# Two output-projection loads moved ahead of the last V load in a decode kernel bound by its loads

## Chip, cores, metric

The kernel runs on one core of one Trainium2 chip. The metric is the device time of one execution in microseconds (us); a profile gives the span of one execution, which is about 1.3 us shorter than the time.

## The reference

One token goes through one transformer block: adaptive layer norm, attention of 32 query heads over 4 cached K/V heads of 65,536 positions in the reference (128 wide), output projection, and a gated feed-forward.

```python
mod = (_silu(c) @ w_mod).reshape(...)              # sa, ca, ga, sb, cb, gb
h = _layernorm(x) * (1 + ca) + sa
x = x + ga * attention(h, k_cache, v_cache, wq, wo)
h = _layernorm(x) * (1 + cb) + sb
x = x + gb * ((gelu(h @ w_gate) * (h @ w_up)) @ w_down)
```

With one token, every weight and every cache row is used once. The profile counts 185.6 MB read, of which 134 MB are the caches (32 loads of 4,096 KB). How fast these bytes come in is the main question of this kernel.

## The kernel before

The kernel keeps ten slots of 16 KB per partition in on-chip memory. A K or V load (4,096 KB, two chunks of 64 positions per partition) takes two neighbouring slots: K loads take turns on slots 0 to 3, V loads on slots 4 to 7. Slots 8 and 9 carry weights only, before and after the attention. The loads are planned as one list. One engine (SyncE) issues them strictly in the order of that list, each once its slots have been freed:

```python
def issue_ready():
    while issued[0] < len(loads):
        j = loads[issued[0]]
        if any(q.freed[t] is None for q, t in j.prev):
            return
        SP.wait(*(q.freed[t] for q, t in j.prev))        # the slots' former readers are done
        sp.dma_start(j.view, j.src).then_inc(j.tok[0], 16)
        issued[0] += 1
# ... cut ...
for i in range(0, NC + UN, UN):                          # NC = 32 chunks, UN = 2 per load
    if i < NC:
        j_k[i] = plan_load(kv_src(kh, i, UN), ..., i % SITES, ...)
    if i >= UN:
        j = i - UN
        j_v[j] = plan_load(kv_src(vh, j, UN), ..., SITES + j % SITES, ...)
tail = iter([8, 9, 0, 1, 2, 4, 3, 5, 6, 7, 8, 9] + [0, 1, 2, 4, 3, 5, 6, 7])
j_o = [(plan_load(wo_v[:, k:k + 8, :], flat(8, D), next(tail)), k, 8) for k in range(0, HQ, 8)]
# ... then w_gate (4 loads), w_up (4), w_down (3 large, 3 small) on the next slots of tail
```

So the last V load comes behind the last K load and the V load before it, and it needs slots 6 and 7, which the value products (PV) of chunks 26 and 27 must free. Everything behind it in the list waits too. At the end come the merging of the chunks' softmax, the product with wo, a layer norm, and the feed-forward's three products. Each of these takes its weights load by load.

## Time and profile before

| | before |
|---|---|
| time, first three runs | 445.17 us median (444.18 to 446.75) |
| profiled execution | 444.85 us, span 443.5 us |
| load queue q1, share of 16 DMA engines' span | 97.9% |
| TensorE (PE) busy | 72% |

These lines of the page of the kernel before give the span, the mean busy share of the DMA engines in 40 slices of 11.1 us (in tenths), what they moved in each slice, and the queues (packets, MB, share):

```profile
span 443.5 us, 16706 instructions
...
DMA  8999999999999999999999999999999899999995
GB/s 328 430 423 425 451 424 433 434 429 428 426 431 429 434 441 427 431 434 431 429 446 429 429 434 432 429 443 432 429 437 429 358 378 421 419 425 421 426 426 217
...
q1 hardware_dynamic: 10864, 185.60, 97.9%
q8 instruction: 25, 0.41, 0.3%
```

The queue is full nearly everywhere. Of the inner slices only the 32nd and 33rd are low, with 358 and 378 GB/s. The next fence cuts that place into windows of 2 us. The columns are busy time (instructions) per engine, then the granted clock of PE, the busy share of the DMA engines, and GB/s:

```profile
core 0: us, PE busy (x) PEld busy (x) DVE busy (x) ACT busy (x) POOL busy (x), PEclk, DMA share, GB/s
350.00:352.00 2.00, 2.00 (x49) 2.00 (x46) 1.07 (x2) 0.00 (x0) 0.00 (x0) 0.66 0.95 410
352.00:354.00 2.00, 2.00 (x67) 2.00 (x64) 1.80 (x2) 0.00 (x0) 0.00 (x0) 1.00 0.57 246
354.00:356.00 2.00, 2.00 (x50) 1.88 (x48) 0.45 (x2) 1.92 (x2) 0.00 (x0) 1.00 0.36 98
356.00:358.00 2.00, 2.00 (x61) 2.00 (x59) 1.66 (x3) 2.00 (x15) 0.00 (x0) 1.00 1.06 393
```

The transfer falls to 246 and to 98 GB/s, where about 427 is usual. The reason stands in the timeline of the issuing engine (start, duration, what was issued, how many), here for the last K load, the last two V loads, and wo behind them:

```profile
321.99 0.33 SPq L217 DMA_DIRECT2D slots<-in_A_k_cache_dram  x1
335.16 20.13 SPq L217 DMA_DIRECT2D slots<-in_A_v_cache_dram  x2
355.33 1.97 SPq L217 DMA_DIRECT2D slots<-in_A_wo_dram  x4
357.34 18.24 SPq L217 DMA_DIRECT2D slots<-in_B_w_gate_dram  x4
```

Merged lines hide the gap: the 20.13 us of the two V loads are two issues of 0.33 us with a wait between them. A narrower window of the same timeline shows the second one alone:

```profile
354.96 0.33 SPq L217 DMA_DIRECT2D slots<-in_A_v_cache_dram  x1
```

The list of the queue's own waits (total us, times, longest) names what held it, the PV product on line 489:

```profile
SPq L217 <- PE b L489: 177.1, 14, 19.5
```

The longest wait of that line, 19.5 us, is the one from 335.5 to 354.96. In this time nothing was issued, although slots 8 and 9 were free. Last, the tail on PE (start, duration, group, idle time before it and what ended it):

```profile
367.30 1.85 PE L489 MATMUL b<-p_sb,slots 128*128 128x8 bf16 x64 [0.42 <-DVE o_all L532]
...
378.68 3.78 PE L320 MATMUL kt_ps<-o_pk,slots 128*128 128x1 bf16 x128 [0.28 <-DVE o_pk L635]
...
387.86 1.86 PE L320 MATMUL kt_ps<-o_pk,slots 128*128 128x1 bf16 x64 [3.04 <-DMA slots<-in_A_wo_dram]
...
396.36 2.02 PE L320 MATMUL kt_ps<-h_col,slots 128*128 128x1 bf16 x56 [1.29 <-DMA slots<-in_B_w_gate_dram]
...
409.26 2.02 PE L320 MATMUL kt_ps<-h_col,slots 128*128 128x1 bf16 x56 [2.25 <-DMA slots<-in_B_w_up_dram]
...
440.72 0.37 PE L320 MATMUL kt_ps<-u_col,slots 128*128 128x1 bf16 x8 [0.24 <-DMA slots<-in_B_w_down_dram]
```

Read the brackets: the last wo load, a gate load, an up load and the last piece of w_down are each waited for; the lines left out between them look the same. The tail is a stream of loads with a little work at its end.

One more view is needed, which no page prints. Each of the 62 loads shows 16 increments of its semaphore (992 in all), and the trace keeps the time of each. I read them as one per DMA engine: between 100 and 340 us 16 packets of q1 are in flight in 221 of the 240 us (15 in 7 us, 17 or more in 12 us, from overlaps of 3 to 4 ns), and at over 99% of the starts another packet ends within 4 ns. The trace names no engine; "engine" stands for one of these 16 chains of packets below. First and last increment of some loads of the kernel before, read out of the trace:

```
load              first     last   spread
V, last but one  351.62   355.37     3.75
V, last          366.56   367.04     0.48
wo, last         386.02   387.81     1.79
w_down, last     437.62   440.67     3.05
```

The consumer starts behind the last increment: the last wo group at 387.86 (increment at 387.81), the last w_down group at 440.72 (440.67).

The spread grows where a 16 KB packet of the instruction queue q8 falls (25 of them, called fetches below). While one is in flight, mostly only 15 packets of q1 are (at 24 of the 25; the last falls where the queue drains). Behind the one at 368.84, which took 0.96 us, a q1 packet of 16 KB took 1.08 us where 0.61 is usual, and between the loads that landed at 367.04 and 373.12 one increment moved out: the largest lag grew from 0.48 to 1.69 us, the next one is 0.50.

### The profile page before, as it was taken

To read this page: it belongs to the slowest core of one execution; us is meant where nothing else is said; L and a number is where in the kernel's file an instruction comes from. 1 tells how busy PE (TensorE), PEld (TensorE's weight loads), DVE (VectorE), ACT (ScalarE), POOL (GpSimd) and SP (SyncE) were. 2 spreads that over 40 slices of the span, in tenths; PEclk is the share of its full clock that TensorE was granted. 3 is DMA by queue.
4 is the path that set the end of the run, shared out by engine and by line. 5 is a ranking of instruction groups with operands and counts; after the bars stand their busy time and mean duration, and the time that the engine had idled before them with its cause. 6 is when DMAs were issued, how large, how long until landed. Compare 5 with 4: busy or idle time off the path is not lost.

```text
span 443.5 us, 16706 instructions
## 1 busy us (share of the span) xinstructions
PE 320.2 (72%) x7849; PEld 311.2 (70%) x7849; DVE 165.0 (37%) x282; ACT 142.7 (32%) x548; POOL 3.7 (1%) x21
## 2 busy tenths in 40 slices
PE   2333428959789995977999698797979894654434
PEld 1333428859789995977999687797968894554434
DVE  1000016716454662644456354454635454010000
ACT  1000003633434743436154352734335272000000
POOL 2000000000000000000000000000000000000000
PEclk9999999968886995988589696978969695555555
DMA  8999999999999999999999999999999899999995
GB/s 328 430 423 425 451 424 433 434 429 428 426 431 429 434 441 427 431 434 431 429 446 429 429 434 432 429 443 432 429 437 429 358 378 421 419 425 421 426 426 217
DMA packets 10927, 186.07 MB, mean 420 GB/s; under 512 B 1040, under 2 KB 1040, under 8 KB 3472
## 3 DMA queue, kind: packets, MB, share of 16 engines
q1 hardware_dynamic: 10864, 185.60, 97.9%
q8 instruction: 25, 0.41, 0.3%
q14 instruction: 6, 0.05, 0.0%
q10 hardware_dynamic: 32, 0.00, 0.0%
HBM read 185.60 MB, written 0.00 MB: 418 GB/s over the span
## 4 chain that ended last, share of the span: by engine, by line
DMA 61%; PE 35%; issue 2%; SPq 1%; ACT 0%; DVE 0%
DMA slots<-in_A_k_cache_dram 39%; PE kt_ps L421 21%; DMA slots<-in_B_w_up_dram 6%; PE sc_ps L443 6%; DMA slots<-in_A_wo_dram 6%; DMA slots<-in_B_w_down_dram 5%; PE b L489 5%; DMA slots<-in_w_mod_dram 5%; SPq L217 1%; PE b L467 1%; PE kt_ps L320 1%; ACT kt_sb L524 0%; PE b L457 0%; PE b L676 0%; DVE y_row L678 0%
## 5 line engine op out<-in xcount | busy, mean ns | idle before, releaser
L421 PE MATMUL kt_ps<-ident,slots 128*128 128x128 bf16 x2048 | 162.3, 243 | 42.4 <-DMA slots<-in_A_k_cache_dram 36.7
L421 PEld LDWEIGHTS kt_ps<-ident,slots 128*128 128x128 bf16 x2048 | 140.2, 110 | 44.3 <-DMA slots<-in_A_k_cache_dram 29.8
L524 DVE COPY kt_sb<-kt_ps 128x2048 bf16<-128x2048 bf16 x96 | 117.5, 1224 | 110.4 <-PE kt_ps L421 110.1
L524 ACT ACTIVATE kt_sb<-kt_ps 128x2048 bf16<-128x2048 bf16 x32 | 60.1, 1877 | 218.3 <-PE kt_ps L421 218.3
L555 ACT ACTIVATE p_sb<-sc_ps,mneg 128x64 bf16<-128x64 f32 x256 | 83.5, 562 | 3.6 <-DVE mneg L550 3.5
L555 ACT ACTIVATION_READ_ACCUMULATOR p_sb<-sc_ps,mneg 128x1 f32 x256 | 77.2, 367 | 0.0
L489 PE MATMUL b<-p_sb,slots 128*128 128x8 bf16 x2048 | 69.0, 167 | 3.6 <-issue 2.4
L443 PE MATMUL sc_ps<-q_buf,kt_sb 128*128 128x8 bf16 x2048 | 66.9, 167 | 1.6 <-issue 1.6
L489 PEld LDWEIGHTS b<-p_sb,slots 128*128 128x128 bf16 x2048 | 62.9, 97 | 4.5 <-issue 2.5
L443 PEld LDWEIGHTS sc_ps<-q_buf,kt_sb 128*128 128x128 bf16 x2048 | 64.2, 98 | 1.7 <-issue 1.7
L320 PE MATMUL kt_ps<-h_col,slots 128*128 128x1 bf16 x448 | 16.2, 172 | 17.2 <-DMA slots<-in_B_w_up_dram 9.4
L320 PEld LDWEIGHTS kt_ps<-h_col,slots 128*128 128x128 bf16 x448 | 15.6, 118 | 17.9 <-DMA slots<-in_B_w_up_dram 9.7
L320 PE MATMUL sc_ps<-s_col,slots 128*128 128x1 bf16 x384 | 11.5, 165 | 15.9 <-DMA slots<-in_w_mod_dram 15.9
L320 PEld LDWEIGHTS sc_ps<-s_col,slots 128*128 128x128 bf16 x384 | 11.0, 105 | 16.4 <-DMA slots<-in_w_mod_dram 16.4
L543 DVE TENSOR_REDUCE m_col<-sc_ps 128x8 f32<-128x512 f32 x32 | 21.8, 681 | 1.9 <-PE sc_ps L443 1.9
L548 DVE TENSOR_REDUCE mg<-b 8x1 f32<-8x128 f32 x32 | 8.9, 279 | 26.1 <-PE b L457 26.1
L320 PE MATMUL sc_ps<-h_col,slots 128*128 128x1 bf16 x256 | 7.4, 165 | 12.5 <-DMA slots<-in_A_wq_dram 12.5
L320 PEld LDWEIGHTS sc_ps<-h_col,slots 128*128 128x128 bf16 x256 | 7.1, 104 | 12.8 <-DMA slots<-in_A_wq_dram 9.2
L320 PE MATMUL kt_ps<-u_col,slots 128*128 128x1 bf16 x224 | 6.9, 165 | 9.7 <-DMA slots<-in_B_w_down_dram 9.7
L320 PEld LDWEIGHTS kt_ps<-u_col,slots 128*128 128x128 bf16 x224 | 6.4, 104 | 10.2 <-DMA slots<-in_B_w_down_dram 7.1
L467 PE MATMUL b<-negi,mg 8*128 8x8 f32 x64 | 13.0, 272 | 0.7 <-DVE mg L548 0.7
L467 PEld LDWEIGHTS b<-negi,mg 8*128 8x128 f32 x64 | 10.0, 195 | 3.4 <-DVE mg L548 1.1
(74 smaller groups left out, 62.4 us busy)
## 6 DMA issues: line engine op xcount, KB each, us to landing
slots<-in_A_k_cache_dram SPq DMA_DIRECT2D x16, 4096.0 KB, 23.2
slots<-in_A_v_cache_dram SPq DMA_DIRECT2D x16, 4096.0 KB, 20.2
slots<-in_w_mod_dram SPq DMA_DIRECT2D x8, 1536.0 KB, 18.8
slots<-in_A_wq_dram SPq DMA_DIRECT2D x4, 2048.0 KB, 37.1
slots<-in_A_wo_dram SPq DMA_DIRECT2D x4, 2048.0 KB, 24.4
slots<-in_B_w_gate_dram SPq DMA_DIRECT2D x4, 1792.0 KB, 36.3
slots<-in_B_w_up_dram SPq DMA_DIRECT2D x4, 1792.0 KB, 29.2
slots<-in_B_w_down_dram SPq DMA_DIRECT2D x3, 2048.0 KB, 30.4
```

The lines of the kernel that those rows point to most:

```text
L217: sp.dma_start(j.view, j.src).then_inc(j.tok[0], 16)
L320: ins = pe.matmul(bank[:, j:j + 1], w, rhs[:, k0 + kk:k0 + kk + 1], start=first, stop=True, skip_group_check=True,)
L421: ins = pe.transpose(kt_ps[:, half * 2048 + t * P:half * 2048 + (t + 1) * P], j_k[i - i % UN].view[:, i % UN * CH + b * TB + t, :], ident[ ...
L443: ins = pe.matmul(sc_ps[:, base + n * REP:base + (n + 1) * REP], kt_sb[:, j % 2, n, :], q_buf[:, j % SITES, :], start=True, stop=True,)
L467: ins = pe.matmul(b6[:, 256:256 + REP], mg8[:, j % 2:j % 2 + 1].to_broadcast([REP, P]), negi[:, :], start=True, stop=True,)
L489: ins = pe.matmul(b7[:, s * REP:(s + 1) * REP], j_v[j - j % UN].view[:, j % UN * CH + n, :], p_sb[:, s, n, :], start=(n == 0), stop=(n == ...
L524: ev[i % SITES][b].done(act.activation(dst, src, ACT.Copy) if E_ is AC else dve.tensor_copy(dst, src))
L543: m1[s].done(dve.tensor_reduce(m_col[:, j % 2, :].unsqueeze(2), scv, AX.X, ALU.max))
L548: m2[s].done(dve.tensor_reduce(mg8[:, j % 2:j % 2 + 1], b6[0:REP, 32:32 + P], AX.X, ALU.max))
L555: ins = act.activation(p_sb[:, s, :, h], scv[:, h, :], ACT.Exp, bias=mneg[:, j, h:h + 1], scale=scale, accum_out=z_all[:, j, h:h + 1],)
```

## The change

The intent is to use the wait: the first two wo loads go to slots 8 and 9, which are free, so they can be issued ahead of the last V load and keep the queue fed. In addition the later weights take the K slots (0 to 3) ahead of the V slots (4 to 7). Bytes, instructions and arithmetic stay the same.

```diff
--- before.py
+++ after.py
@@ -247,16 +247,22 @@
         head = [8, 9, 0, 1, 2, 4, 3, 5, 6, 7, 8, 9]
         j_mod = [(plan_load(wmod_v[:, k:k + 1, :], flat(1, M6), head[k]), k, 1) for k in range(KD)]
         j_q = [(plan_load(wq_v[:, k:k + 2, :], flat(2, HQ * DH), head[KD + k // 2]), k, 2) for k in range(0, KD, 2)]
+        tail = iter([8, 9] + 2 * [0, 1, 2, 3, 4, 5, 6, 7, 8, 9])
+
+        def plan_o(k):
+            return (plan_load(wo_v[:, k:k + 8, :], flat(8, D), next(tail)), k, 8)
+
         j_k, j_v = {}, {}
         for i in range(0, NC + UN, UN):
             if i < NC:
                 j_k[i] = plan_load(kv_src(kh, i, UN), flat(UN * CH, DH), i % SITES, kfill[i % SITES // UN], UN)
+            if i == NC:
+                j_o = [plan_o(k) for k in range(0, 16, 8)]
             if i >= UN:
                 j = i - UN
                 j_v[j] = plan_load(
                     kv_src(vh, j, UN), flat(UN * CH, DH), SITES + j % SITES, vfill[j % SITES // UN], UN)
-        tail = iter([8, 9, 0, 1, 2, 4, 3, 5, 6, 7, 8, 9] + [0, 1, 2, 4, 3, 5, 6, 7])
-        j_o = [(plan_load(wo_v[:, k:k + 8, :], flat(8, D), next(tail)), k, 8) for k in range(0, HQ, 8)]
+        j_o += [plan_o(k) for k in range(16, HQ, 8)]
         j_g = [(plan_load(wg_v[:, k:k + 2, :], flat(2, F), next(tail)), k, 2) for k in range(0, KD, 2)]
         j_u = [(plan_load(wu_v[:, k:k + 2, :], flat(2, F), next(tail)), k, 2) for k in range(0, KD, 2)]
         j_d = []
```

## The prediction

> **What bounds it now.** The loads. The page shows queue q1 busy 97.9% of the 16 DMA engines' span, 185.6 MB at a mean 420 GB/s. PE is busy 72%, and waits for every down-projection load (the chain of waits closes with 23.6 us of w_down in flight). Apart from the start and the end, only slices 32 and 33 (343 to 366 us) are low: 358 and 378 GB/s.
>
> **The dip.** In the order of time, the last K load is issued at 321.99 and the V load before the last at 335.16. Then the issuing engine waits 19.5 us for PV to free slots 6 and 7, issues the last V load at 354.96, and wo behind it from 355.33. Slots 8 and 9, for two wo loads, have long been free. The queue runs dry: 246 GB/s in 352-354, 98 GB/s in 354-356, against about 427. That is roughly 3.1 us of transfer.
>
> **But the engines do not run dry together.** The semaphore records give 16 increments per load, one per DMA engine[...]. For the V load before the last they spread from 351.62 to 355.37, 3.75 us; a load counts only when the slowest engine is done. About half of the engines lie 2.9 to 3.75 behind. The spread grows where a 16 KB instruction fetch (q8, 25 of them, 0.88 to 0.97 us each) takes an engine's turn. The pause resets it: the last V load lands with 0.48 us of spread (366.56 to 367.04); by the end it is 3.05 again.
>
> With loads spaced 9.68 us per 4 MB, the slowest engine lost 367.04 - 9.68 - 355.37 = 2.0 us in the pause, the fastest 5.3 us. If the same engines are hit by the later fetches, only the slowest engine's 2.0 us count, and the end's spread grows from 3 to about 5 us.
>
> **What the change does.** wo[0] and wo[1] (4 MB, 9.8 us) go into the queue behind the V load before the last and fill the pause. The last V load lands after them: about 355.4 + 9.75 + 9.7 = 374.8 instead of 367.04. PV of the last two chunks ends near 379 (371.9 now), and the wo product starts near 386 (378.7), 6.8 us of softmax merging later, as now. All four wo loads have landed by then, so its four groups of 64 matmuls run together (7.5 us): end 393.4 against 389.7. h2 comes near 396.8 instead of 393.0. Gate loads then land near 390, 394, 398.5, 403; with 2.03 us per group PE has caught up at the last gate load or the first up load. The queue holds about 30 us of work then, so slots freed 4 us later don't starve it. The new slot order frees the gate loads' slots in time (354 to 366 us).
>
> **Predicted.** DMA stream's last landing moves from 440.67 to about 438.7: minus 2.1 us, half a per cent. 443.1 us, range 441.5 to 444.7. Faster by over 2%: 1%; same: 98%; slower: 1%.
>
> **What would show it.** No slice under 415 GB/s near 350; the last V load landing near 375; wo product starting near 386 without waits between its groups; PE waiting on loads again from the up projection on; spread of the last load near 4 to 5 us; end tail unchanged (2.8 us after the last landing).
>
> **What would make it wrong.** If later fetches hit engines that were ahead, the gain nears 3.1 us or more. If the wo product's later start outlasts the gate loads, or a slot freed late starves the queue, the gain shrinks or vanishes.

## The result

| | before | changed |
|---|---|---|
| median of six runs, same chip | 445.29 us (444.18 to 446.75) | 443.02 us (442.56 to 443.43) |
| ratio | | 0.9943, 95% interval 0.9922 to 0.9964 |
| profiled span | 443.5 us | 441.8 us |
| last V load, issued / landed | 354.96 / 367.04 us | 354.14 / 376.29 us |
| wo product, start / end | 378.68 / 389.72 us | 387.23 / 395.93 us |
| last weight load landed | 440.67 us | 438.99 us |
| spread of that load over the engines | 3.05 us | 5.76 us |

A ratio here is the mean time of one kernel's fast runs over the mean of the other's fast runs of the same rounds, so it is not quite the ratio of the medians. The changed kernel is half a per cent faster.

The same lines of the page, now of the changed kernel:

```profile
span 441.8 us, 16706 instructions
...
DMA  8999999999999999999999999999999999999994
GB/s 329 428 426 425 452 426 429 430 426 431 439 429 429 421 427 429 433 433 448 430 427 434 427 430 434 433 451 428 427 433 427 430 436 420 424 425 424 423 425 167
...
q1 hardware_dynamic: 10864, 185.60, 98.2%
q8 instruction: 25, 0.41, 0.3%
```

The two low slices are gone (430 and 436 GB/s). One new number is at the end: the last slice moved 167 GB/s, before it was 217. The windows around the former pause:

```profile
core 0: us, PE busy (x) PEld busy (x) DVE busy (x) ACT busy (x) POOL busy (x), PEclk, DMA share, GB/s
350.00:352.00 2.00, 2.00 (x67) 2.00 (x64) 1.53 (x2) 0.00 (x0) 0.00 (x0) 1.00 1.06 459
352.00:354.00 2.00, 2.00 (x62) 1.99 (x58) 1.22 (x3) 0.74 (x1) 0.00 (x0) 1.00 1.01 434
354.00:356.00 2.00, 2.00 (x44) 1.90 (x41) 0.69 (x3) 2.00 (x8) 0.00 (x0) 1.00 0.84 360
356.00:358.00 2.00, 2.00 (x57) 2.00 (x55) 2.00 (x3) 1.64 (x12) 0.00 (x0) 1.00 0.98 418
```

No window is near empty any more. The issuing engine of the changed kernel:

```profile
322.30 0.33 SPq L217 DMA_DIRECT2D slots<-in_A_k_cache_dram  x1
335.51 0.33 SPq L217 DMA_DIRECT2D slots<-in_A_v_cache_dram  x1
335.88 0.91 SPq L217 DMA_DIRECT2D slots<-in_A_wo_dram  x2
354.14 0.33 SPq L217 DMA_DIRECT2D slots<-in_A_v_cache_dram  x1
354.51 0.91 SPq L217 DMA_DIRECT2D slots<-in_A_wo_dram  x2
355.46 18.43 SPq L217 DMA_DIRECT2D slots<-in_B_w_gate_dram  x4
```

Two wo loads now leave at 335.88, straight behind the V load at 335.51. The last V load still leaves at about 354. And the tail on PE:

```profile
376.33 1.87 PE L495 MATMUL b<-p_sb,slots 128*128 128x8 bf16 x64 [10.19 <-DMA slots<-in_A_v_cache_dram]
...
387.23 5.49 PE L326 MATMUL kt_ps<-o_pk,slots 128*128 128x1 bf16 x200 [0.29 <-DVE o_pk L641]
394.30 1.63 PE L326 MATMUL kt_ps<-o_pk,slots 128*128 128x1 bf16 x56 [1.58 <-issue]
...
399.26 6.76 PE L326 MATMUL kt_ps<-h_col,slots 128*128 128x1 bf16 x198 [2.00 <-DVE h_col L373]
406.58 2.90 PE L326 MATMUL kt_ps<-h_col,slots 128*128 128x1 bf16 x82 [0.56 <-issue]
411.74 2.03 PE L326 MATMUL kt_ps<-h_col,slots 128*128 128x1 bf16 x56 [2.26 <-DMA slots<-in_B_w_up_dram]
...
439.03 0.37 PE L326 MATMUL kt_ps<-u_col,slots 128*128 128x1 bf16 x8 [0.24 <-DMA slots<-in_B_w_down_dram]
```

The last PV now waits 10.19 us for its V load. The wo product starts 8.5 us later than before, but it runs without a wait for a load, and so do the five groups of 56 matmuls from 399.26 to 409.5: the four of the gate and the first of up (198 + 82 matmuls). From the second up load at 411.74 on, PE waits for loads as before. Two idle times, 1.58 us inside the wo product and 0.56 us inside the gate groups, are put down to "issue", not to a load; the bullet on the wo product below returns to them. So the later attention costs nothing: PE waits for loads again 30 us before the end.

What is left to explain is the size. In the pause of before, about 3 us of average transfer were missing, and the time fell by 1.7 us between the two profiled executions (444.85 to 443.15). The 16 increments of the last load show where the difference went. Offsets of the 16 engines from the first one, sorted, in us:

```
before, first at 437.62: 0.00 0.16 0.16 0.20 0.20 0.24 0.25 0.44 1.59 1.61 1.64 1.67 1.69 1.72 1.88 3.05
changed, first at 433.23: 0.00 0.13 0.38 0.40 0.42 0.53 1.17 2.01 3.58 3.59 3.99 4.22 4.24 4.32 4.39 5.76
```

The mean over the engines is 437.62 + 1.03 = 438.65 before and 433.23 + 2.45 = 435.68 in the changed kernel: the average engine ends 2.97 us earlier, as the filled pause would have it. The last engine ends only 1.68 us earlier (440.67 to 438.99). The time follows the last engine (1.68 us against 1.70 us between the two profiled executions).

### The profile page after: what moved, and what is told of

It reads as the page before. It is cut to its first block, busy times and chain, and to the rows that moved or that the text cites. A ratio compares the mean times of both kernels' runs of the same rounds, so it can differ in the third digit from the quotient of the medians.

```text
span 441.8 us, 16706 instructions
## 1 busy us (share of the span) xinstructions
PE 319.6 (72%) x7849; PEld 311.0 (70%) x7849; DVE 165.0 (37%) x282; ACT 142.8 (32%) x548; POOL 3.7 (1%) x21
## 4 chain that ended last, share of the span: by engine, by line
DMA 57%; PE 37%; issue 2%; DVE 2%; SPq 1%; ACT 1%
DMA slots<-in_A_k_cache_dram 35%; PE kt_ps L427 22%; PE sc_ps L449 7%; PE b L495 7%; DMA slots<-in_B_w_up_dram 6%; DMA slots<-in_B_w_down_dram 5%; DMA slots<-in_A_v_cache_dram 5%; DMA slots<-in_w_mod_dram 5%; PE b L473 1%; SPq L217 1%; PE b L463 1%; DVE kt_sb L530 1%; PE kt_ps L326 1%; ACT kt_sb L530 0%; DVE m_col L549 0%
```

## The experiments

The theory: the gain is the pause, counted on the slowest DMA engines, and the eight slowest are slow because instruction fetches take turns on them (which engine a fetch hits is not shown). Rivals: the slot order does it; the later attention eats part of the gain; the average transfer counts; the lag of the engines is random. Each ratio is to the kernel before, run in the same session on one chip. Its median was 444.06 us (e1 to e4), 444.52 (e5 to e8), 444.61 (e9 to e11) and 444.74 (e12). The four calls ran on four different chips.

### e1: the slot order alone

```diff
-tail = iter([8, 9, 0, 1, 2, 4, 3, 5, 6, 7, 8, 9] + [0, 1, 2, 4, 3, 5, 6, 7])
+tail = iter([8, 9] + 2 * [0, 1, 2, 3, 4, 5, 6, 7, 8, 9])      # in the kernel before
```

> Kernel before with the new slot order alone; all wo loads stay behind the last V load. Theory (the gain is the filled pause of the load queue): the pause near 352 to 356 us stays, the last V load lands near 367 with under 0.6 us of spread, time equal to before, ratio 1.000 (0.997 to 1.003). Rival (the slot order frees slots earlier and so feeds the queue): ratio 0.995 or less.

Measured: 444.36 us, ratio 1.0013 (0.9997 to 1.0030). The pause stays, as two of its windows show (columns as above):

```profile
352.00:354.00 2.00, 2.00 (x64) 1.99 (x60) 1.33 (x2) 0.39 (x1) 0.00 (x0) 1.00 0.61 262
354.00:356.00 2.00, 2.00 (x48) 1.90 (x47) 0.57 (x3) 2.00 (x6) 0.00 (x0) 1.00 0.89 246
```

The last V load lands at 366.44 with 0.35 us of spread. The slot order does nothing to the time.

### e2: the early loads alone

```diff
-tail = iter([8, 9] + 2 * [0, 1, 2, 3, 4, 5, 6, 7, 8, 9])
+tail = iter([8, 9, 0, 1, 2, 4, 3, 5, 6, 7, 8, 9] + [0, 1, 2, 4, 3, 5, 6, 7])      # in the changed kernel
```

> Changed kernel with the old slot order in the tail; only the two early wo loads remain. Theory: no pause, spread of the last load near 5.8 us, time as the changed kernel, 443.0 us, ratio 0.995 (0.992 to 0.998). Rival (slot order): ratio 1.000.

Measured: 443.03 us (five runs within 443.00 to 443.07), the time of the changed kernel. The ratio was 0.9979 (0.9966 to 0.9992), inside the expected range but closer to 1 than its middle, because the kernel before ran faster (444.06 us). The spread of the last load was 6.38 us. So the early loads carry the whole gain, and what varies is the kernel before; e9 to e11 return to this.

### e3: one early load

```diff
-    j_o = [plan_o(k) for k in range(0, 16, 8)]
+    j_o = [plan_o(k) for k in range(0, 8, 8)]
```

(The other three wo loads follow behind the last V load.)

> Only one wo load (2 MB, about 4.9 us of the queue) ahead of the last V load. Theory: 4.9 us behind the fastest DMA engine's 351.6 reaches 356.5, past the issue of the last V load at about 355, so the pause is just filled and the slowest engine never idles: 443.0 us, ratio 0.995, last V load about 5 us earlier than in the changed kernel (near 371), wo product from about 382. Rival (about 1 us of the 3.1 us average is lost because the wo product starts 8 us later): this version would be faster than the changed one by about 0.5 to 1 us, 442.0 to 442.5, ratio 0.993.

Measured: 443.17 us, ratio 0.9982 (0.9969 to 0.9995). The last V load landed at 371.49, 4.8 us earlier than in the changed kernel, and the time was the same. The rival that the late wo product costs something is not supported.

### e4: all four early

```diff
-    j_o = [plan_o(k) for k in range(0, 16, 8)]
+    j_o = [plan_o(k) for k in range(0, HQ, 8)]
```

> All four wo loads ahead of the last V load. Theory: the last V load lands about 10 us later than in the changed kernel (near 386), the wo product starts near 397, h2 near 409, PE runs the gate groups back to back and has caught up by the third or fourth up load; last landing unmoved at about 439: 443.0 us, ratio 0.995. Rival (the late wo product costs time): 444 to 447 us, ratio 0.998 to 1.004.

Measured: 441.82 us, ratio 0.9952 (0.9939 to 0.9965). It was 1.2 us faster than e2 on the same chip, which neither the theory nor its rival had expected. The tail on PE:

```profile
386.02 1.87 PE L494 MATMUL b<-p_sb,slots 128*128 128x8 bf16 x64 [20.46 <-DMA slots<-in_A_v_cache_dram]
...
396.93 5.49 PE L325 MATMUL kt_ps<-o_pk,slots 128*128 128x1 bf16 x200 [0.28 <-DVE o_pk L640]
...
428.65 3.50 PE L325 MATMUL kt_ps<-u_col,slots 128*128 128x1 bf16 x123 [1.08 <-issue]
435.14 2.95 PE L325 MATMUL kt_ps<-u_col,slots 128*128 128x1 bf16 x96 [2.99 <-DMA slots<-in_B_w_down_dram]
```

The attention ends as late as expected (the wo product starts at 396.93), and PE catches up with the loads only at the third down load (435.14). The last weight load landed at 437.68 with 5.07 us of spread, instead of 438.99 with 5.76. The idle time of 1.08 us marked "issue" is one of four in e4's tail, 5.2 us in all. The trace's packets of q8, the instruction queue, offer a reason for the gain. In the changed kernel nine 16 KB fetches start behind 360 us, the last at 434.98, ahead of the last landings, and there one engine lies 1.4 us behind all others. In e4 the ninth starts at 437.21, 0.47 us ahead of the last landing; I take this as too late to hold up the loads, and PE's later progress as what moved it. Neither is shown. e7 tests whether such fetches cost time.

### e5: where the engines' queues end

Fifteen tiny loads on 1 to 15 partitions follow the last weight load of the changed kernel. I assumed that a load on n partitions adds one engine to those of the load on n - 1.

```diff
+for n in range(1, 16):
+    psem = nc.alloc_semaphore(f"probe{n}")
+    ptile = sb(f"probe{n}", [n, 64], dt.bfloat16)
+    sp.dma_start(ptile[:, :], A_wq[0:n, 0:64]).then_inc(psem, 16)
```

> Changed kernel with fifteen tiny loads (1 to 15 partitions of 128 bytes, never read) queued behind the last weight load[...]. Theory (the instruction fetches always take turns on the same eight engines): the ends fall into two groups, about eight engines early (0 to 2 us after the first) and eight late (3.6 to 5.8 us), and the same eight by number as a block or a regular pattern. Rival (the lag is spread over the engines at random): no pattern, intermediate values for most. Time near 443.

Measured: 443.01 us in its one run. The load on n partitions shows n late increments, besides one at once. Comparing each load's increments with those of the load before gives one new time per load. I read it as the end of one more engine's queue; the numbers are the order of the probe, 0 for the load on one partition, and e11 and e12 use them too:

```
engine   0      1      2      3      4      5      6      7
end    433.2  435.1  433.2  434.4  433.9  437.2  436.8  433.4
engine   8      9      10     11     12     13     14     15
end    433.3  437.6  437.7  437.5  439.0  437.6  437.2  early: among the first eight of the last weight load
```

The engines fall into two groups of eight: 5, 6 and 9 to 14 end late, the others early, and engine 12 ends last.

### e6: half a load early

```diff
-    j_o = [plan_o(k) for k in range(0, 16, 8)]
+    j_o = [plan_o(0, 4)]                                   # 1 MB; plan_o(k, n) loads n heads
 ...
-j_o += [plan_o(k) for k in range(16, HQ, 8)]
+j_o += [plan_o(4, 8), plan_o(12, 8), plan_o(20, 8), plan_o(28, 4)]
```

> Only 1 MB of wo (2.4 us of the queue) ahead of the last V load. Theory (a load counts when its slowest engine is done): the fast engines still idle for about 2 us (351.7 + 2.4 = 354.1 against a restart near 356), the slow ones, 3.7 us behind, do not; so the page still shows a dip of about 1 us of average transfer, but the time is that of the changed kernel, 443.0 us, within 0.3 us. Rival (the gain is the average transfer lost in the pause): 0.6 to 1 us slower than the changed kernel of this call, 443.6 to 444.0 us.

Measured: 443.21 us (442.84 to 443.83), ratio 0.9968 (0.9949 to 0.9987); the changed kernel (e8) had 442.73 us. The windows show a smaller dip than expected:

```profile
352.00:354.00 2.00, 2.00 (x50) 1.88 (x48) 0.81 (x2) 1.19 (x1) 0.00 (x0) 1.00 1.03 442
354.00:356.00 2.00, 2.00 (x46) 2.00 (x46) 1.09 (x2) 2.00 (x11) 0.00 (x0) 1.00 0.89 320
```

In the trace six engines had run dry and started again between 354.65 and 355.35; the other ten had not. The last landing was 439.13, against 438.82 in e8. This agrees with the theory, but the medians differ by 0.5 us, more than the 0.3 us expected and nearly as much as the rival's 0.6, with overlapping ranges. As a timing, e6 is inconclusive.

### e7: fewer instructions behind the pause

The result is wrong on purpose: `matvec` leaves out 560 of 928 matmuls of the tail (the trace has 7,289 matmuls instead of 7,849; the expectation below says 568). The loads are unchanged.

```diff
-for kk in range(nk):
+for kk in range(min(nk, cut or nk)):      # cut=2 for wo and w_down, cut=1 for w_gate and w_up
```

> Wrong result on purpose: the changed kernel with 568 of the 928 tail matmuls left out (two of eight heads of each wo load, one of two gate and up row blocks, two row blocks of each down load), so about four to five instruction fetches fewer behind 367 us; all loads as in the changed kernel. Theory (each fetch sets one of eight engines back by about 1.4 us, and the ninth behind the pause hits an engine twice): at most five or six fetches are left, none hits an engine a second time, the last landing's spread falls from 5.8 to about 4.4 us, the time by 1.3 us to 441.7 us. Rival (fetches cost only their average share, 0.95 us of one engine in sixteen each): 0.3 us faster at most.

Measured: 441.78 us, ratio 0.9934 (0.9916 to 0.9953), against 442.73 us of the changed kernel. The page's line of the instruction queue:

```profile
q8 instruction: 21, 0.34, 0.3%
```

Four of 25 fetches are gone, and five instead of nine start behind 360 us. The last weight load landed at 437.55, 1.27 us ahead of e8, with 5.08 us of spread instead of 6.46; no engine stands out from the slow group any more. The rival allowed at most 0.3 us. Leaving out these matmuls, and four fetches with them, was worth about 1 us. From the last landing to the end of the run it took 4.17 us in e7 and in e8, so the shorter computation itself gained nothing there.

### e8: the changed kernel again

(No edit.)

> The changed kernel again, for comparison on the same chip. Theory: 443.0 us, nine fetches behind 365 us, spread of the last load near 5.8 us; ratio to before 0.995 to 0.998, as the length of the pause in before varies with the granted clock.

Measured: 442.73 us, ratio 0.9960 (0.9939 to 0.9982), nine fetches behind 360 us, spread 6.46 us. As expected.

### e9 and e10: a later issue of the last V load

```diff
+j_v[NC - UN].prev.append((j_k[NC - UN], 1))     # also waits for the last K chunk's transposes
```

e9 is the kernel before with this line:

> Kernel before, with the last V load made to wait in addition for the transposes of the last K chunk (about 361 us instead of 355). Theory: all DMA engines have run dry by 355.4, so each further us of pause costs one us: plus 6.0 us (5.4 to 6.8), about 450.5 us, ratio 1.0135. Rival (the pause is hidden behind the attention's own work): plus 2 us or less.

e10 is the changed kernel with the same line:

> Changed kernel with the same later issue of the last V load (about 361 us). Theory: the two wo loads hold the fast engines until about 361.3 and the slow ones until about 365, so only the fast ones idle, for a us or two, and the time stays that of the changed kernel, 442.9 us within 0.4. Rival (any delay of the last V load counts): plus 2 to 6 us.

Measured: e9 451.13 us, ratio 1.0136 (1.0103 to 1.0170); e10 443.29 us, ratio 0.9966 (0.9933 to 0.9998). Two of the six runs of e9 took about 455 us, and the profiled one is one of these. Its windows:

```profile
350.00:355.00 5.00, 5.00 (x110) 5.00 (x108) 3.04 (x3) 0.00 (x0) 0.00 (x0) 0.50 0.76 328
355.00:360.00 5.00, 5.00 (x81) 4.87 (x80) 0.86 (x4) 3.83 (x15) 0.00 (x0) 0.50 0.00 0
360.00:365.00 5.00, 5.00 (x123) 5.00 (x122) 3.71 (x5) 0.59 (x5) 0.00 (x0) 0.85 0.00 0
```

Nothing moves for ten microseconds. PE's granted clock was 0.50 up to 360, and the load was issued at 365.49, where about 361 had been expected. In the kernel before, PE did 33 to 34 matmuls in 2 us at a clock of 0.50 (346 to 350 us) and 67 at 1.00 (352 to 354). In e10 the last V load was issued at 360.71, 6.4 us later than in e8, and the last landing stayed (438.86 against 438.82). The two wo loads are a buffer that takes up such a delay.

### e11: the probe on the kernel before

The fifteen tiny loads of e5 in the kernel before.

> Kernel before with the same fifteen tiny loads behind its last weight load. Theory (always the same eight engines): engines 5, 6 and 9 to 14 end about 1.3 to 3.1 us after the others, as eight hits since the pause would have it, the others within 0.6 us of the first. Rival (which engines are hit changes from program run to program run): another set.

Measured: 446.60 us in its one run. The late engines are again 5, 6 and 9 to 14, and again engine 12 is the last of all (about 442.6, the others of the group about 441). The early eight lie within 0.8 us of each other, a little more than expected. So the same eight, by the probe's order, are late in both kernels.

That fetches go round eight engines is inferred, with further support in the traces that the experiments did not use: how long the fetches took repeats after eight. The nine behind 360 us, in ns:

```
before   960 967 947 886 879 942 933 921 961
changed  960 960 951 879 878 935 933 924 971
```

The sixteen fetches ahead of 360 us show nearly the same series twice (in the kernel before only 968 and 960 stand where 942 and 933 do here). In e7 the series is the same but starts at another place, so that e7 may have changed which engines the fetches hit, and not only their number. The ninth fetch falls on the turn of the first in this series, and the largest lag grows there: in the changed kernel from 4.48 to 5.82 us (loads landed at 435.17 and 437.75), and in the last load it is 5.76 us, 1.4 us behind the next engine.

The run of e11 was slow for another reason, which is useful: PE's granted clock was 0.50 from 345 to 360 us, and the last V load left at 356.49 only. The profiled executions of the kernels with the pause line up, and those without it don't move:

| profiled execution | last V load issued | last landing | time |
|---|---|---|---|
| e1, with pause | 354.50 | 440.23 | 444.40 |
| before, with pause | 354.96 | 440.67 | 444.85 |
| e11, with pause | 356.49 | 442.45 | 446.60 |
| e9, with pause | 365.49 | 451.39 | 455.56 |
| changed | 354.14 | 438.99 | 443.15 |
| e8, changed again | 354.35 | 438.82 | 442.99 |
| e10, changed, later issue | 360.71 | 438.86 | 443.03 |

From e1 to e9 the issue moves by 10.99 us and the time by 11.16 us. In the changed kernel 6.4 us of delay cost nothing. This probably is also why the kernel before scatters over 2.6 us in its first six runs and the changed one over 0.9 us: before, each execution pays for the pace of PE ahead of that one issue. The runs without a profile can't be checked for it, and the changed kernel has one outlier as well (444.16 us in e8).

### e12: bytes moved from slow engines to five fast ones

In e4, one 256 KB piece of the last w_down block is issued as 26 pieces of at most five partitions. In e5 the load on five partitions showed five late increments, read as engines 0 to 4 of the probe's order, all in the early group there (433.2 to 435.1).

```diff
-    sp.dma_start(j.view, j.src).then_inc(j.tok[0], 16)
+    for r in range(0, P, j.rows):                     # rows=5 for one piece, else 128
+        e = min(r + j.rows, P)
+        sp.dma_start(j.view[r:e], j.src[r:e]).then_inc(j.tok[0], 16)
```

> All four wo loads early, and one of the last 256 KB pieces of w_down is loaded in 26 pieces of at most five partitions, which by the probe run on the first five DMA engines only[...]. Theory (the end is set by the eight engines that the fetches set back): these get 16 KB less each, 0.6 us, the first five 35 KB more, 1.3 us; the spread of the last load falls from 5.0 to about 4.4 us and the time from 441.8 to about 441.2 us. Rival (the end is set by bytes and small descriptors): 441.8 us or slower.

Measured: 442.98 us, ratio 0.9957 (0.9935 to 0.9980), 1.2 us slower than e4 had been. A miss, on the rival's side. e4 was on another chip, and its ratio was nearly the same (0.9952), so that the size of the loss is not shown. The increments of the small pieces begin at 431.28 and end at 438.36: the pieces took 7 us in sequence where I had estimated under 2 us per engine from their bytes (about 52 KB at a sixteenth of 427 GB/s). In the last load only three engines are still early: five of the early eight, as many as the pieces were meant for, have lost their lead of several us. Nor was it a clean test, because ahead of that piece the slow engines already lay 0.8 us later than in e4 (the third large w_down load landed at 435.93, not 435.10). That the slow engines set the end without this edit is not refuted, but the remedy brought no gain.

## Why the prediction was right

Time: predicted 443.1 us (441.5 to 444.7), measured 443.02 us. That the two agree within 0.1 us is partly luck: 443.1 is 2.1 us below the first median of before (445.17), while the profiled executions differ by 1.7 us. With the median 444.06 the same subtraction would have given 442.0, and e2 measured 443.03. Point by point:

- *The pause and its cause.* Right. The early loads alone bring the time (e2), the slot order alone nothing (e1), and the pause costs one for one (e9, e11 and the table).
- *Only the slowest engine's idle time counts.* Right, with sizes: predicted 2.0 us of about 3.1; the last landing moved by 1.68 us, the mean of the engines by 2.97 us. The spread of the last load became 5.76 us, a little above the predicted 5.
- *The same engines are hit by the later fetches.* This was an assumption. e5 and e11 show the same eight places of the probe's order late in both kernels, with 12 the last (439.0 and about 442.6); in e7, with four fetches and 560 matmuls fewer, the last landing came 1.27 us earlier. The link of one fetch to one engine is inferred, from the lags and from the durations that repeat after eight: the trace doesn't name the engine of a packet.
- *The last V load near 374.8.* It landed at 376.29. Across one fetch, at 368.39, the largest lag grew from 2.97 to 4.40 us (loads landed at 365.18 and 376.29); the sum had left that out.
- *The wo product from 386, end at 393.4, h2 (the input of the gate and up products) near 396.8.* Measured 387.23, 395.93 and 399.26. The missed 1.5 us came from the V load, another 1.58 us from an idle time inside the product that the profile puts down to "issue". PE stops at this same matmul in the traces of e2 to e6, e8, e10 and e12 too (1.57 to 1.86 us), and each time goes on 1.3 to 1.5 us after a 16 KB fetch has ended; in e7, with fewer matmuls, it doesn't stop. That it waits for instructions there is my guess; no run was made to test it. PE had caught up at the first up load, as predicted (that group could start about 0.1 us after its load), and e3 and e4 show that the slack was larger still.
- *Tail.* Predicted 2.8 us from the last landing to the span's end; measured 441.8 - 438.99 = 2.8.

What the prediction lacked is that the gain is not a constant. It was worked out from one profile of before; the kernel before had medians between 444.06 and 445.29 us, and ratios of the changed kernel or its equal (e2, e8) lay between 0.9943 and 0.9979. The changed kernel's medians stayed within 442.7 to 443.1.

Of the versions tried that compute the right result, e4 is the fastest (441.82 us). Its extra 1.2 us seem to come from where the last instruction fetch happens to fall; e7 measured an earlier end with four fetches and 560 matmuls fewer, and for e4 it is only argued.

## What to carry to other kernels

In a kernel that is bound by its loads, look for the one load in the issue order that waits for a slot, and put loads that need no slot ahead of it; one early load of sufficient size was as good as two (e3), and two also took up a delay of 6.4 us (e10). Count the gain of a filled pause on the slowest DMA engine, not on the average transfer: while the queue was dry, the engines that lagged caught up (the spread fell from 3.75 to 0.48 us), and that part of the pause was already free. When the last loads set the end, as here, look at every engine's own queue: an instruction fetch takes its time from the same 16 chains (mostly 15 packets of q1 in flight during one), and with 560 matmuls and four fetches fewer the last load landed 1.27 us earlier (e7 against e8).

## What the traces showed besides

- Instruction fetches: 25 packets of 16,384 bytes on q8. In the tail of the changed kernel PE stopped for 1.58 and 0.56 us and went on 1.4 to 1.6 us after a fetch had ended (in e4 four such stops add up to 5.2 us), though this did not set the end there. With the load queue full each fetch took 0.88 to 0.97 us (kernels before and changed), and the largest lag grew by 1.2 to 1.4 us at the first and at the ninth of those behind 360 us (0.48 to 1.69 and 1.91 to 3.10 us before, 2.97 to 4.40 and 4.48 to 5.82 changed).
- The first packets after a dry queue: fifteen of the sixteen first packets of 32 KB took 1.48 to 2.02 us instead of 1.21 (kernel before, 355.9 to 356.5).
